# Attention and a squared-ReLU MLP in one kernel: the moving operands of both MLP products read as two interleaved halves

## Chip, cores, metric

The kernel runs on one NeuronCore of a Trainium2 chip. The metric is device time in microseconds, from one launch; what the host does before and after (turning arrays round, putting columns in order) is not in it.

## The reference

Two attention steps with 32 inducing points over 4 x 12480 tokens of 128 channels, then an MLP with 2048 hidden units on all 49920 tokens.

```python
def mab(q, kv):
    s = scale * (q @ kv.transpose(0, 2, 1))
    s = s - s.max(-1, keepdims=True)
    a = np.exp(s)
    a /= a.sum(-1, keepdims=True) + 1e-09
    return a @ kv
h = mab(I, x)
return mab(x, h).astype(np.float32)
...
h = x @ w_in
r = np.maximum(h, 0.0)
g = s * (r * r) + b
return (g @ w_out).astype(np.float32)
```

## The kernel before

The tokens are cut into 104 blocks of 480 (`BLK`; 26 for each of 4 batches). A token is a column, a channel a partition. The second attention step isn't multiplied out: `attend` leaves, for each block, the attention weights split into a high and a low float32r part and spread over 128 partitions (`a2t`), and `wst` holds the inducing points' values already multiplied by `w_in`, split in the same way. One product of `wst` (128 of 2048 hidden units at a time) with `a2t` then gives `h`.

**A pair** is two such products, 256 hidden units of one block, 8 pairs to a block, 832 in all. Its steps, each recorded at the line named:

- L737, TensorE: two matmuls `h <- a2t, wst` into one of three PSUM tiles `h` (two banks each). The moving operand is `a2t`, 480 columns.
- L752 (ScalarE) or L754 (VectorE): `r = relu(h)`, kept in SBUF.
- L802, ScalarE: `g1 = r * r`, rounded to float32r, for one pair (960 columns a partition) or for two at once (1920).
- L765, VectorE: the product `S = relu(h) * r` without that rounding. For a pair of kind "P" it goes to an SBUF tile `g`, for kind "D" back over `h` in PSUM.
- L779: `g2 = S - g1`, the rounding error of the square: on GpSimd for kind P, on VectorE for kind D.
- L827, TensorE: `x += w_hi * g1 + w_lo * g1` (four matmuls a pair) and `x += w_hi * g2` (two), into one of two banks `x` that collect a block. The moving operands are `g1` and `g2`, 480 columns each.
- L835 or L837: when a block is complete, scale and bias into `ob`, and a store.

In the names of the profile the buffer numbers are left out, so `g`, `g1` and `g2` all stand there as `g`. So both MLP products together are 104 x 16 x 4 = 6656 matmuls of 128 x 128 x 480, and each has its own weights loaded ahead of it.

**Work beside it.** While batch b's blocks run, the attention of batch b + 1 (`scores`, `top`, `values`, `points`, `w_tiles`) and the next `attend` are put between, at the block counts in `ATTEND_AT`, `SCORES_AT` and so on. They use the bank `x` that the running block does not.

**What sets the order.** `Plan` is a list scheduler that runs while the program is built. Each unit of work names its engine, its estimated time and an urgency; the constants at the top (`M_U`, `R_U`, `SQ`, `S_U`, `C_U`, `OUT_HI`, `OUT`) are added to a pair's number to make urgencies, `MM` is its estimate for one matmul, and `SLIP` and `WEIGHT` say how far urgency may hold an engine back. The order that comes out is fixed in the program. Kind P or D is also chosen there: a pair is P while the planner's backlog of GpSimd work is under `POOL_Q` and a tile `g` is free. Nothing is chosen on the chip.

**The opening** (up to about 61 us) does the first attention step for batch 0, brings in and narrows the weights, and keeps TensorE busy with warm-up matmuls (L959), whose results are not used. They run on a tile of zeros, with moving operands of eight forms, four matmuls each, in the order of the list `shapes`:

```python
plain = warm_sb[:, 0:BLK]
shapes = [
    plain,
    warm_sb.rearrange("p (t n) -> p n t", t=2)[:, 0:BLK // 2, :],
    warm_sb.rearrange("p (n t) -> p n t", t=2)[:, :, 0],
    warm_sb[:, 0:BLK // 2].unsqueeze(2).broadcast_to([P, BLK // 2, 2]),
    warm_sb.rearrange("p (t a c) -> p a t c", t=2, c=16)[:, 0:BLK // 32],
    warm_16[:, 0:BLK],
    warm_sb[:, 4:4 + BLK],
    warm_sb.rearrange("p (t a c) -> p a t c", t=2, c=4)[:, 0:BLK // 8],
]
```

The second form takes columns 0, 480, 1, 481 and so on; the last takes four columns from one half, then four from the other.

Of the kernel before, what the change touches and what calls it, by code (L numbers as in the profile page):

```python
# [9 lines left out]

F32 = mybir.dt.float32
F32R = mybir.dt.float32r
BF16 = mybir.dt.bfloat16
I32 = mybir.dt.int32
U32 = mybir.dt.uint32
AF = mybir.ActivationFunctionType
# [4 lines left out]
P = 128  # L21
T = 120
NQ = 4
BLK = T * NQ
# [3 lines left out]
TH = 8  # L28
WC = 512

POOL_Q = 4.228
POOL_L = 2.231


LAT = 0.180
SLIP = 0.159
WEIGHT = 0.0272
LEAN = {"ACT": -0.50}
R_LEAN = {"DVE": 0.00}


M_U = -5.604
R_U = 2.437
SQ = 3.369
MM = 0.2165
S_U = -1.313
C_U = -5.000
OUT_HI = 1.632
OUT = 1.982
FRONT = 0.379  # L50
FIRST = -200.0
SPREAD = -50.0
# [20 lines left out]
class Plan:  # L73
# [13 lines left out]
    def _step(self, unit, urgency, ready=None):  # L87
# [3 lines left out]
        if want is not None:  # L91
            eng, us, *waits = want
            if not isinstance(eng, dict):
                engs, lean = {eng: us}, LEAN
            elif isinstance(us, dict):
                engs, lean = eng, us
            else:
                engs, lean, waits = eng, LEAN, [us, *waits]
            more = sum(w for w in waits if isinstance(w, float))
# [16 lines left out]
    def run(self):  # L116
        ev = self.events
        while self.units:
            able = {}
            for u in self.units:  # L120
# [7 lines left out]
                )  # L128
                able.setdefault(eng, []).append((at + WEIGHT * urgency, at, engs[eng], u))
            assert able, [(u[3], u[4]) for u in self.units]  # L130
            picks = []
            for eng, steps in able.items():
                best = min(steps, key=lambda x: x[0])

                fill = [x for x in steps if x[1] + x[2] <= best[1] + SLIP]
                picks.append((*min(fill or [best], key=lambda x: x[0])[1:], eng))
# [8 lines left out]
def tile_attn_relu2(ctx: ExitStack, tc: tile.TileContext, xT, xN, indT, w_in, w_out, s_rep, b_rep, outT):  # L145
    nc = tc.nc
    B, _, N = xT.shape
# [23 lines left out]


    bank = [ps_x.tile([P, 512], F32, name=f"x{n}") for n in range(2)]

    def copy(out, in_):

        if plan.eng == "ACT":
            nc.scalar.copy(out=out, in_=in_)  # L178
        else:
            nc.vector.tensor_copy(out=out, in_=in_)  # L180
# [3 lines left out]
    def ring(name, bufs):  # L184

        n = taken.get(name, 0)
        taken[name] = n + 1
        if n < bufs:
            plan.events[name, n - bufs] = 0.0
        return n, (name, n - bufs)  # L190

    def next_free(name, bufs):

        n = taken.get(name, 0)
        return 0.0 if n < bufs else plan.events.get((name, n - bufs), math.inf)
# [522 lines left out]
    def place(k):  # L718
        blk, pr = divmod(k, NPAIR)
        return *divmod(blk, NBLK), pr  # L720
# [5 lines left out]
    def pair(k):  # L726

        b, blk, pr = place(k)
        n = pr % 2
        turn, free = ring("h", 3)  # L730
        yield "PE", 2 * MM, M_U, free, ("a2t", b, blk), ("wst", b, 2 * pr * P // WC), ("mm1", k - 1)
        wst, (A, A_turn) = st[b]["wst"], a2t[b, blk]
        h = ps_h.tile([P, 2, 512], F32, name="h")
        hv = h[:, :, 0:BLK]
        for u in range(2):
            c = 2 * pr + u
            nc.tensor.matmul(h[:, u, 0:BLK], wst[:, c * P:(c + 1) * P], A, start=True, stop=True)  # L737
        plan.set(("mm1", k))
        if pr == NPAIR - 1:
            plan.set(("a2t", A_turn))  # L740
        if k + 1 < total:
            plan.spawn(pair(k + 1), k + 1, plan.end)
        if n == 0:
            quad[k] = {"r": ring("r", 2), "g1": ring("g1", 4), "g1_uses": 4, "r_uses": 4, "R": []}
        q = quad[k - n]
        yield dict(ACT=0.855, DVE=1.08), R_LEAN, R_U, q["r"][1]
        if n == 0:
            q["r_t"] = ew.tile([P, 4, BLK], F32, name="r", bufs=2)
        half = slice(2 * n, 2 * n + 2)
        r = q["r_t"][:, half, :]  # L750
        if plan.eng == "ACT":
            nc.scalar.activation(out=r, in_=hv, func=AF.Relu)  # L752
        else:
            nc.vector.tensor_scalar(out=r, in0=hv, scalar1=0.0, scalar2=None, op0=ALU.max)  # L754
        plan.set(("R", k))
        q["R"].append((n, plan.end))
        if len(q["R"]) == 1:
            plan.spawn(square(k - n), k + SQ, plan.end + LAT)
        yield "DVE", 1.07, S_U
        wait = max(0.0, pool_work[0] - plan.end)  # L760
        kind = "P" if wait < POOL_Q and next_free("g", 4) <= plan.start else "D"
        if kind == "P":
            g_turn, _ = ring("g", 4)
        g = hv if kind == "D" else ew.tile([P, 2, BLK], F32, name="g", bufs=4)
        nc.vector.scalar_tensor_tensor(out=g, in0=hv, scalar=0.0, in1=r, op0=ALU.max, op1=ALU.mult)  # L765
        plan.set(("S", k))
        if kind != "D":
            plan.set(("h", turn))
        q["r_uses"] -= 1
        if q["r_uses"] == 0:  # L770
            plan.set(("r", q["r"][0]))
        if kind == "P":
            pool_work[0] = max(pool_work[0], plan.end) + POOL_L
        n2, free2 = ring("g2", 8)
        yield ("Pool", POOL_L, ("Q", k), free2) if kind == "P" else ("DVE", 1.07, C_U, ("Q", k), free2)
        hi = q["g1_t"][:, half, :]
        g2 = ew.tile([P, 2, BLK], F32R, name="g2", bufs=8)
        eng = nc.gpsimd if kind == "P" else nc.vector
        eng.tensor_tensor(out=g2, in0=g, in1=hi.bitcast(F32), op=ALU.subtract)  # L779
        plan.set(("h", turn) if kind == "D" else ("g", g_turn))  # L780
        g1_used(q)
        ops = [(w_hi[:, 2 * pr + u, :], g2[:, u, :]) for u in range(2)]
        plan.spawn(out_part(k, ops, 2 * MM, "w_split", lambda: plan.set(("g2", n2))), k + OUT, plan.end + LAT)

    def g1_used(q, n=1):
        q["g1_uses"] -= n
        if q["g1_uses"] == 0:
            plan.set(("g1", q["g1"][0]))

    def square(k0):  # L790
# [12 lines left out]
        for i in range(lo, hi):  # L803
# [3 lines left out]
            plan.spawn(  # L807
                out_part(k0 + i, ops, 4 * MM, "w_split", lambda: g1_used(q)), k0 + i + OUT_HI, plan.end + LAT
            )
        if q["R"]:  # L810
            plan.spawn(square(k0), k0 + 1 + SQ, q["R"][0][1] + LAT)
        q["r_uses"] -= hi - lo
# [3 lines left out]
    def out_part(k, ops, us, weights, used):  # L816

        b, blk, pr = place(k)
        blk_g = b * NBLK + blk
        yield "PE", us, (weights, 2 * pr * P // WC), ("front", blk_g - 1) if blk_g else "first", ("ob", blk_g - 2)  # L820
        o = bank[blk_g % 2][:, 0:BLK]
        left = parts.setdefault(blk_g, 2 * NPAIR)
        first = left == 2 * NPAIR
        left -= 1
        parts[blk_g] = left
        for n, (w, g) in enumerate(ops):
            nc.tensor.matmul(o, w, g, start=first and n == 0, stop=left == 0 and n == len(ops) - 1)  # L827
        used()
        if left:
            return  # L830
        front_work(blk_g + 1)
        yield dict(ACT=0.64, DVE=0.69), 0.0, "bias"
        ob = p2.tile([P, BLK], F32, name="ob")
        if plan.eng == "ACT":
            nc.scalar.activation(out=ob, in_=o, func=AF.Identity, bias=bias, scale=s_sb)  # L835
        else:
            nc.vector.tensor_scalar(out=ob, in0=o, scalar1=s_sb, scalar2=bias, op0=ALU.mult, op1=ALU.add)  # L837
        c0 = b * N + blk * BLK
        nc.sync.dma_start(out=outT[:, c0:c0 + BLK], in_=ob)
        plan.set(("ob", blk_g))  # L840
# [68 lines left out]
    left = [0, 0, 0]  # L909
# [7 lines left out]
    def opening():  # L917
# [18 lines left out]
    warm_turn, _ = ring("g2", 8)  # L936
    warm_sb = ew.tile([P, 2 * BLK], F32R, name="g2", bufs=8)
    nc.gpsimd.memset(warm_sb.bitcast(F32), 0.0)
    warm_16 = warm_sb.bitcast(BF16)
    plain = warm_sb[:, 0:BLK]  # L940
    shapes = [
        plain,
        warm_sb.rearrange("p (t n) -> p n t", t=2)[:, 0:BLK // 2, :],
        warm_sb.rearrange("p (n t) -> p n t", t=2)[:, :, 0],
        warm_sb[:, 0:BLK // 2].unsqueeze(2).broadcast_to([P, BLK // 2, 2]),
        warm_sb.rearrange("p (t a c) -> p a t c", t=2, c=16)[:, 0:BLK // 32],
        warm_16[:, 0:BLK],
        warm_sb[:, 4:4 + BLK],
        warm_sb.rearrange("p (t a c) -> p a t c", t=2, c=4)[:, 0:BLK // 8],
    ]  # L950
    shapes = itertools.cycle([x for x in shapes for _ in range(4)])

    def warm(n, ps, *waits):

        for _ in range(n):
            yield "PE", 0.22, *waits
            x = next(shapes)
            w = (warm_16 if x.dtype == BF16 else warm_sb)[:, 0:P]
            nc.tensor.matmul(ps()[:, 0:BLK], w, x, start=True, stop=True)  # L959

    def keep_warm(ps, *waits):

        while plan.events.get(("a2t", 0, 0), math.inf) > plan.end + 0.3:
            yield from warm(1, ps, *waits)
        plan.set(("g2", warm_turn))
# [27 lines left out]
_OUT = "out_dram"  # L993
# [33 lines left out]
```

## Time and profile before

| | |
|---|---|
| median of 3 runs | 1614.33 us (1614.32 to 1616.04) |
| profiled execution | 1615.43 us, its span 1613.6 us |
| granted TensorE clock | 0.998 of full speed |
| matmuls of L737 / L827 | 1664 / 4992 |
| pairs of kind P / D | 682 / 150 |
| relus on ScalarE / VectorE | 661 / 171 |
| squares of one pair / of two | 808 / 12 |

The span runs from the first to the last instruction of the profiled execution, so a sum made from its rows is a sum for that execution. In the rows below a group's two numbers behind the bar are its busy time in us and the mean of one in ns; behind the second bar stands the engine's idle time just before the group, and what ended most of it. Matmuls overlap, so their mean (380 ns) is not their pace; the pace is the distance between starts. PE is TensorE, DVE VectorE, ACT ScalarE, POOL GpSimd.

### The profile page before, as it was taken

The numbers are of one execution on the slowest core, as the hardware profiler recorded it, in microseconds if no ns is written. First come the engines' busy times: TensorE is split into PE (matmuls) and PEld (weight loads), VectorE is DVE, ScalarE is ACT, GpSimd is POOL, SyncE is SP. The second block draws the span as 40 slices with busy tenths as digits, with TensorE's granted clock in tenths as the row PEclk, the third lists the DMA queues.
The fourth block names the chain that finished last, engine by engine and source line by source line (L and its number), as shares of the span: only waits on it lengthen the run. The fifth ranks groups of instructions, "written<-read, shape, count | busy, mean of one in ns | idle before, by whom it ended". The sixth has DMA issues, their size and how long they took to land.

```text
span 1613.6 us, 24901 instructions
## 1 busy us (share of the span) xinstructions
PE 1596.5 (99%) x8223; PEld 1300.7 (81%) x8223; DVE 1462.3 (91%) x1590; ACT 1514.9 (94%) x1812; POOL 1541.4 (96%) x701
## 2 busy tenths in 40 slices
PE   8899999999999999999999999999999999999998
PEld 5578788888887878888887788888888888888787
DVE  5899999989999999999999989989998999998996
ACT  7599999999999999999999999999999999999997
POOL 1699999999999999999999999999999999999998
PEclk9999999999999999999999999999999999999999
DMA  8222313313233222231223322322311112112100
GB/s 299 64 89 89 104 62 117 99 40 89 63 104 101 70 88 91 90 103 52 74 92 99 100 84 74 117 80 62 92 46 62 38 49 68 31 52 66 56 31 19
DMA packets 59312, 129.42 MB, mean 80 GB/s; under 512 B 11952, under 2 KB 38576, under 8 KB 59184
## 3 DMA queue, kind: packets, MB, share of 16 engines
q1 hardware_dynamic: 59184, 127.83, 25.2%
q8 instruction: 67, 1.10, 0.3%
q14 instruction: 61, 0.50, 0.1%
HBM read 73.52 MB, written 25.56 MB: 61 GB/s over the span
## 4 chain that ended last, share of the span: by engine, by line
PE 96%; ACT 1%; DVE 1%; DMA 0%; issue 0%; POOL 0%; POOLq 0%; SPq 0%; ACTq 0%
PE x L827 67%; PE h L737 23%; PE x L662 2%; PE x L612 1%; PE x L573 1%; DMA xt<-in_xT_dram 0%; PE h L959 0%; PE h L414 0%; PE x L362 0%; ACT r L752 0%; PE h L382 0%; POOL g L779 0%; ACT e L392 0%; DVE g L765 0%; PE h L397 0%
## 5 line engine op out<-in xcount | busy, mean ns | idle before, releaser
L779 POOL TENSOR_TENSOR g<-g,g 128x960 fp32r<-128x960 f32 x682 | 1523.7, 2293 | 18.6 <-DVE g L765 12.0
L827 PE MATMUL x<-g,w_hi 128*128 128x480 f32 x3328 | 1058.7, 381 | 1.5 <-POOL g L779 1.5
L765 DVE SCALAR_TENSOR_TENSOR g<-h,r 128x960 f32<-128x960 f32 x682 | 768.1, 1147 | 61.7 <-ACT r L752 50.6
L802 ACT ACTIVATE g<-r 128x960 fp32r<-128x960 f32 x820 | 806.8, 1016 | 18.3 <-DVE r L754 4.7
L827 PEld LDWEIGHTS x<-g,w_hi 128*128 128x128 f32 x3328 | 622.8, 188 | 113.5 <-POOL g L779 9.3
L752 ACT ACTIVATE r<-h 128x960 f32<-128x960 f32 x661 | 626.8, 967 | 43.6 <-PE h L737 29.2
L827 PE MATMUL x<-g,w_lo 128*128 128x480 f32 x1664 | 633.1, 380 | 2.4 <-ACT g L802 1.5
L737 PE MATMUL h<-a2t,wst 128*128 128x480 f32 x1664 | 505.7, 385 | 0.5 <-DVE g L765 0.3
L737 PEld LDWEIGHTS h<-a2t,wst 128*128 128x128 f32 x1664 | 305.4, 188 | 85.6 <-issue 28.4
L827 PEld LDWEIGHTS x<-g,w_lo 128*128 128x128 f32 x1664 | 312.6, 188 | 56.2 <-issue 4.9
L754 DVE TENSOR_SCALAR r<-h 128x960 f32<-128x960 f32 x171 | 196.6, 1150 | 19.8 <-PE h L737 16.8
L765 DVE SCALAR_TENSOR_TENSOR h<-h,r 128x960 f32<-128x960 f32 x150 | 173.7, 1158 | 9.4 <-ACT r L752 8.6
L779 DVE TENSOR_TENSOR g<-h,g 128x960 fp32r<-128x960 f32 x150 | 172.6, 1151 | 7.9 <-ACT g L802 2.4
L835 ACT ACTIVATE ob<-x,bias,s_sb 128x480 f32<-128x480 f32 x103 | 77.0, 748 | 9.4 <-PE x L827 8.7
L310 POOL TENSOR_TENSOR w_in_sb<-w_in_sb,g 128x512 f32<-128x512 f32 x4 | 5.3, 1333 | 26.0 <-DVE g L305 26.0
L662 PE MATMUL x<-xt,hT 128*32 128x480 f32 x208 | 28.3, 578 | 0.5 <-DVE hT L501 0.5
L694 DVE TENSOR_TENSOR hl<-x,hl 128x480 fp32r<-128x480 f32 (+1 forms) x28 | 18.3, 655 | 7.3 <-ACT hl L178 6.7
L310 POOL TENSOR_TENSOR wst<-wst,g 128x512 f32<-128x512 f32 x4 | 5.8, 1466 | 19.1 <-DVE g L305 19.1
L612 PEld LDWEIGHTS x<-xn,eT 128*32 128x32 f32 (+1 forms) x630 | 16.9, 109 | 7.0 <-DVE eT L607 3.7
L612 PE MATMUL x<-xn,eT 128*32 128x128 f32 (+1 forms) x630 | 22.5, 275 | 0.0
L669 DVE STREAM_TRANSPOSE x<-x 128x480 f32<-128x480 f32 (+1 forms) x28 | 19.3, 690 | 3.4 <-PE x L662 3.3
L573 PE MATMUL x<-xt,ind_sb 128*32 128x480 f32 x156 | 21.2, 578 | 0.0
(116 smaller groups left out, 417.8 us busy)
## 6 DMA issues: line engine op xcount, KB each, us to landing
xt<-in_xT_dram SPq DMA_DIRECT2D x102, 480.0 KB, 4.4
a2t<-hl SPq DMA_DIRECT2D x416, 60.0 KB, 2.0
out_dram<-ob SPq DMA_DIRECT2D x104, 240.0 KB, 2.0
xn<-in_xN_dram SPq DMA_DIRECT2D x18, 512.0 KB, 3.8
xn<-in_xN_dram SPq DMA_DIRECT2D x18, 448.0 KB, 4.4
wst<-whl SPq DMA_DIRECT2D x48, 64.0 KB, 2.0
g<-in_w_in_dram SPq DMA_DIRECT2D x4, 512.0 KB, 6.6
g<-in_w_out_dram SPq DMA_DIRECT2D x4, 512.0 KB, 5.9
```

The lines of the kernel that those rows point to most:

```text
L573: nc.tensor.matmul(ps[M * q:M * (q + 1), 0:BLK], ind_sb, xt[:, q % SB], start=True, stop=True)
L612: nc.tensor.matmul(ps[M * c:M * (c + 1), 0:P], eT[0:rows, n], xn_tiles[b, g, half][0][0:rows, n - half * TH], start=n < P // M, stop=n + P ...
L662: nc.tensor.matmul(ps[M * q:M * (q + 1), 0:BLK], hT[:, 0:M], xt[:, q % SB], start=True, stop=True)
L669: nc.vector.transpose(out=s, in_=s)
L737: nc.tensor.matmul(h[:, u, 0:BLK], wst[:, c * P:(c + 1) * P], A, start=True, stop=True)
L752: nc.scalar.activation(out=r, in_=hv, func=AF.Relu)
L754: nc.vector.tensor_scalar(out=r, in0=hv, scalar1=0.0, scalar2=None, op0=ALU.max)
L765: nc.vector.scalar_tensor_tensor(out=g, in0=hv, scalar=0.0, in1=r, op0=ALU.max, op1=ALU.mult)
L779: eng.tensor_tensor(out=g2, in0=g, in1=hi.bitcast(F32), op=ALU.subtract)
L802: nc.scalar.activation(out=q["g1_t"][:, sl, :], in_=q["r_t"][:, sl, :], func=AF.Square)
L827: nc.tensor.matmul(o, w, g, start=first and n == 0, stop=left == 0 and n == len(ops) - 1)
L835: nc.scalar.activation(out=ob, in_=o, func=AF.Identity, bias=bias, scale=s_sb)
```

## The change

A function `by_turns` reads a tile of 480 columns as two halves by turns: columns 0, 240, 1, 241, and so on. It is put around the moving operand of both products. The result is written without gaps, so `h` has its columns in the new order, and `x` in that order applied twice; everything between works column by column. The host undoes it twice on the output. Besides, the planner's constants have new values, and the warm-up matmuls run through six other forms (40 of them, not 41). Lines behind L176 have numbers 3 higher in the changed kernel (L737 becomes L740, L765 L768, L779 L782, L802 L805, L827 L830).

```diff
-POOL_Q = 4.228
+POOL_Q = 2.9681
...
-SLIP = 0.159
-WEIGHT = 0.0272
-LEAN = {"ACT": -0.50}
-R_LEAN = {"DVE": 0.00}
+SLIP = 0.0319
+WEIGHT = 0.0251
+LEAN = {"ACT": -0.5}
+R_LEAN = {"DVE": -0.008}
...
-SQ = 3.369
-MM = 0.2165
...
-C_U = -5.000
-OUT_HI = 1.632
-OUT = 1.982
+SQ = 1.2698
+MM = 0.2035
...
+C_U = -11.5827
+OUT_HI = 1.9705
+OUT = 0.5153
...
+    def by_turns(x):
+
+        return x.rearrange("p (t n) -> p n t", t=2)
...
-            nc.tensor.matmul(h[:, u, 0:BLK], wst[:, c * P:(c + 1) * P], A, start=True, stop=True)
+            nc.tensor.matmul(h[:, u, 0:BLK], wst[:, c * P:(c + 1) * P], by_turns(A), start=True, stop=True)
...
-            nc.tensor.matmul(o, w, g, start=first and n == 0, stop=left == 0 and n == len(ops) - 1)
+            nc.tensor.matmul(o, w, by_turns(g), start=first and n == 0, stop=left == 0 and n == len(ops) - 1)
...
-    return np.ascontiguousarray(r.results[0][_OUT].T)
+    y = r.results[0][_OUT]
+    for _ in range(2):
+        y = y.reshape(C, B * N // BLK, BLK // 2, 2).transpose(0, 1, 3, 2).reshape(C, B * N)
+    return np.ascontiguousarray(y.T)
```

The new constants move instructions. On VectorE, in the middle of the program, around the end of one `attend` (the transposition of `x`, then `hl`) and a `values` (`eT`, `accb`), the order before is:

```order
L687 STREAM_TRANSPOSE x_86<-x_86 128x480
L765 SCALAR_TENSOR_TENSOR g<-h,r 128x960
L694 TENSOR_TENSOR hl<-x_86,hl 128x480
L765 SCALAR_TENSOR_TENSOR g<-h,r 128x960 x3
L607 STREAM_TRANSPOSE eT<-s 128x480
L754 TENSOR_SCALAR r<-h 128x960
L765 SCALAR_TENSOR_TENSOR g<-h,r 128x960
L623 TENSOR_TENSOR accb<-x_85,accb 128x128
L765 SCALAR_TENSOR_TENSOR g<-h,r 128x960 x2
L765 SCALAR_TENSOR_TENSOR h<-h,r 128x2x480
```

At the same place in the changed kernel, on the same engine:

```order
L690 STREAM_TRANSPOSE x_86<-x_86 128x480
L768 SCALAR_TENSOR_TENSOR g<-h,r 128x960
L697 TENSOR_TENSOR hl<-x_86,hl 128x480
L768 SCALAR_TENSOR_TENSOR g<-h,r 128x960 x2
L757 TENSOR_SCALAR r<-h 128x960
L610 STREAM_TRANSPOSE eT<-s 128x480
L768 SCALAR_TENSOR_TENSOR g<-h,r 128x960
L768 SCALAR_TENSOR_TENSOR h<-h,r 128x2x480
L626 TENSOR_TENSOR accb<-x_85,accb 128x128
L782 TENSOR_TENSOR g_7094<-h,g_7054 128x960
```

Behind the transposition seven products went to `g`, for GpSimd, ahead of the first that stays in `h`; now it is four, and VectorE makes that pair's difference itself (L782). Over the whole program 659 pairs are P and 173 D.

On ScalarE, the end of the program before:

```order
L752 ACTIVATE r<-h 128x960 x2
L802 ACTIVATE g_16089<-r 128x960
L802 ACTIVATE g_16131<-r 128x960
L752 ACTIVATE r<-h 128x960
L802 ACTIVATE g_16131<-r 128x960
L835 ACTIVATE ob<-x_86,bias,s_sb 128x480
```

And in the changed kernel:

```order
L838 ACTIVATE ob<-x_85,bias,s_sb 128x480
L805 ACTIVATE g_16059<-r 128x960
L755 ACTIVATE r<-h 128x960 x2
L805 ACTIVATE g_16059<-r 128x960
L805 ACTIVATE g_16089<-r 128x1920
L838 ACTIVATE ob<-x_86,bias,s_sb 128x480
```

The last two pairs' squares are one instruction of 1920 columns now. Over the program 37 squares are of two pairs and 758 of one (12 and 808 before); ScalarE has 678 relus (661) and VectorE 154 (171).

On TensorE, the last matmuls before, all of L827:

```order
L827 MATMUL x_86<-g_16131,w_lo 128x480
L827 MATMUL x_86<-g_16131,w_hi 128x480
L827 MATMUL x_86<-g_16153,w_hi 128x480 x2
L827 MATMUL x_86<-g_16165,w_hi 128x480 x2
L827 MATMUL x_86<-g_16169,w_hi 128x480 x2
```

And in the changed kernel:

```order
L830 MATMUL x_86<-g_16095,w_hi 128x480 x2
L830 MATMUL x_86<-g_16104,w_hi 128x480 x2
L830 MATMUL x_86<-g_16089,w_lo 128x480
L830 MATMUL x_86<-g_16089,w_hi 128x480
L830 MATMUL x_86<-g_16089,w_lo 128x480
L830 MATMUL x_86<-g_16089,w_hi 128x480
L830 MATMUL x_86<-g_16114,w_hi 128x480 x2
L830 MATMUL x_86<-g_16110,w_hi 128x480 x2
```

Before, three differences of GpSimd (`g_16153`, `g_16165`, `g_16169`) came last. Now two of the last ones are VectorE's (`g_16104`, `g_16114`), and one of GpSimd (`g_16110`) still ends the program.

More of the change, by code (lines that the diff above doesn't have):

```diff
@@ L12 @@
 F32R = mybir.dt.float32r
-BF16 = mybir.dt.bfloat16
 I32 = mybir.dt.int32
@@ L29 @@
 WC = 512
-POOL_Q = 4.228
+POOL_Q = 2.9681
 POOL_L = 2.231
 LAT = 0.180
-SLIP = 0.159
-WEIGHT = 0.0272
-LEAN = {"ACT": -0.50}
-R_LEAN = {"DVE": 0.00}
-M_U = -5.604
-R_U = 2.437
-SQ = 3.369
-MM = 0.2165
-S_U = -1.313
-C_U = -5.000
-OUT_HI = 1.632
-OUT = 1.982
+SLIP = 0.0319
+WEIGHT = 0.0251
+LEAN = {"ACT": -0.5}
+R_LEAN = {"DVE": -0.008}
+M_U = -6.4309
+R_U = 1.8519
+SQ = 1.2698
+MM = 0.2035
+S_U = -1.1474
+C_U = -11.5827
+OUT_HI = 1.9705
+OUT = 0.5153
 FRONT = 0.379
@@ L938, in tile_attn_relu2 @@
     nc.gpsimd.memset(warm_sb.bitcast(F32), 0.0)
-    warm_16 = warm_sb.bitcast(BF16)
-    plain = warm_sb[:, 0:BLK]
     shapes = [
[L942 to L949, printed above, removed]
+        warm_sb[:, 0:BLK].rearrange("p (n t) -> p t n", t=2),
+        warm_sb.rearrange("p (n t) -> p t n", t=2)[:, 0],
+        warm_sb[:, 0:BLK].rearrange("p (t n) -> p n t", t=4),
+        warm_sb[:, 0:BLK].rearrange("p (t n) -> p n t", t=BLK // 4),
+        warm_sb[:, 0:BLK].rearrange("p (t a c) -> p a t c", t=2, c=2),
+        by_turns(warm_sb[:, 0:BLK]),
     ]
@@ L957, in warm @@
             x = next(shapes)
-            w = (warm_16 if x.dtype == BF16 else warm_sb)[:, 0:P]
-            nc.tensor.matmul(ps()[:, 0:BLK], w, x, start=True, stop=True)
+            nc.tensor.matmul(ps()[:, 0:BLK], warm_sb[:, 0:P], x, start=True, stop=True)
     def keep_warm(ps, *waits):
```

## The prediction

> **What bounds the kernel now.** I read the page first, then the long stretch without the opening, then the groups, then single stretches of the time line.
>
> ```profile
> span 1613.6 us, 24901 instructions
> PE 1596.5 (99%) x8223; PEld 1300.7 (81%) x8223; DVE 1462.3 (91%) x1590; ACT 1514.9 (94%) x1812; POOL 1541.4 (96%) x701
> PE 96%; ACT 1%; DVE 1%; DMA 0%; issue 0%; POOL 0%; POOLq 0%; SPq 0%; ACTq 0%
> ...
> core 0: us, PE busy (x) PEld busy (x) DVE busy (x) ACT busy (x) POOL busy (x), PEclk, DMA share, GB/s
> 61.00:1613.60 1552.60, 1544.42 (x7692) 1267.53 (x7690) 1422.19 (x1495) 1476.49 (x1713) 1526.18 (x684) 1.00 0.24 75
> ```
>
> The reader is to see two things. The chain that ended last is TensorE's, 96%. And behind it stands not one idle engine but a second one that is nearly full: from 61 us on GpSimd works 1526.2 of 1552.6 us, 98%. TensorE can gain only until GpSimd becomes the end. DMA, at a share of 0.24, is far off, and the granted clock is 1.00, so no throttle hides in the numbers.
>
> A busy TensorE is not a TensorE at its peak, so I take its pace from where matmuls follow each other without a wait, in the chain of waits:
>
> ```profile
> 467.31 3.49 PE x L827 x16
> 1237.51 4.78 PE x L827 x22
> ```
>
> 3.49 / 16 = 0.2181 and 4.78 / 22 = 0.2173 us: **0.218 us for one product of 480 columns** with a plainly read moving operand.
>
> **The price of the new reading** stands in this trace already, because the warm-up matmuls (L959) take eight forms of moving operand in turn, four of each, in the order of the list `shapes`. The last 13 of the 41, numbers 29 to 41, run in one piece ahead of the first pair. By the list they are four that read runs of 4 columns by turns from two places, four plain, four that take single columns by turns from two halves, and one with a stride of 2. In the chain of waits, then in the time line (start, time until the last one's end, count):
>
> ```profile
> 57.99 3.29 PE h L959 x13
> ...
> 58.32 0.85 PE L959 MATMUL h<-g 128*128 128x480 f32 x3
> ...
> 59.01 1.04 PE L959 MATMUL h<-g 128*128 128x480 f32 x4
> ...
> 59.88 0.97 PE L959 MATMUL h<-g 128*128 128x480 f32 x4
> ...
> 60.69 0.59 PE L959 MATMUL h<-g 128*128 128x480 f32 x1
> ```
>
> The first line is all 13; the others begin with numbers 30, 33, 37 and 41. From start to start: runs of 4, (59.01 - 58.32) / 3 = 0.230; plain, (59.88 - 59.01) / 4 = 0.2175, the pace of the main part; single columns by turns, (60.69 - 59.88) / 4 = **0.2025 us**. Against the 0.218 of the main part that is 0.0155 us less for each.
>
> What these rows don't show is the exact form of the change: there the halves lie 480 columns apart, here 240, and the tiles hold data, not zeros. I bound it by the same rows, 0.2025 below and 0.230 above, and take 0.2025, since the order of reading (one column from either half) is that of the 0.2025 row, and since plain reads cost the same on zeros (0.2175) and on data (0.218). Both ends count for the range.
>
> The Trainium skill, page "SBUF — State Buffer", section "Door 1: The DMA port swizzle", speaks against the change: SBUF has lines of 16 bytes, an access runs at full speed only with two or more hits in a line, and every step to another line is paid for. By that rule a read that changes lines at every column is the worst form of all; here it is the fastest of the three. For this form the trace disagrees with the page.
>
> **Term 1, TensorE.** Both products make 1664 + 3328 + 1664 = 6656 matmuls (L737 and the two rows of L827 in the groups below). 6656 x 0.0155 = 103 us. If TensorE stayed the end, the span would be 1613.6 - 103 = 1510.6 us.
>
> **Term 2, the other engines.** The change sets the planner's numbers anew, and so shares out the elementwise work differently. The rows that price it:
>
> ```profile
> L779 POOL TENSOR_TENSOR g<-g,g 128x960 fp32r<-128x960 f32 x682 | 1523.7, 2293 | 18.6 <-DVE g L765 12.0 <-PE x L827 2.6 <-ACT hl L178 1.1
> L827 PE MATMUL x<-g,w_hi 128*128 128x480 f32 x3328 | 1058.7, 381 | 1.5 <-POOL g L779 1.5
> L802 ACT ACTIVATE g<-r 128x960 fp32r<-128x960 f32 x808 | 785.2, 1004 | 18.1 <-DVE r L754 4.7 <-issue 0.4
> L765 DVE SCALAR_TENSOR_TENSOR g<-h,r 128x960 f32<-128x960 f32 x682 | 768.1, 1147 | 61.7 <-ACT r L752 50.6 <-POOL g L779 6.9
> L827 PE MATMUL x<-g,w_lo 128*128 128x480 f32 x1664 | 633.1, 380 | 2.4 <-ACT g L802 1.5 <-DVE hl L694 0.8
> L752 ACT ACTIVATE r<-h 128x960 f32<-128x960 f32 x661 | 626.8, 967 | 43.6 <-PE h L737 29.2 <-ACT g L802 9.8 <-ACT r L752 1.9
> L737 PE MATMUL h<-a2t,wst 128*128 128x480 f32 x1664 | 505.7, 385 | 0.5 <-DVE g L765 0.3
> L754 DVE TENSOR_SCALAR r<-h 128x960 f32<-128x960 f32 x171 | 196.6, 1150 | 19.8 <-PE h L737 16.8 <-ACT r L752 1.3 <-ACT g L802 0.5
> L765 DVE SCALAR_TENSOR_TENSOR h<-h,r 128x960 f32<-128x960 f32 x150 | 173.7, 1158 | 9.4 <-ACT r L752 8.6
> L779 DVE TENSOR_TENSOR g<-h,g 128x960 fp32r<-128x960 f32 x150 | 172.6, 1151 | 7.9 <-ACT g L802 2.4
> L802 ACT ACTIVATE g<-r 128x1920 fp32r<-128x1920 f32 x12 | 21.8, 1816 | 0.2
> ```
>
> Counted over the whole program in the order of the changed kernel:
> - GpSimd makes 659 differences in place of 682. One costs 1523.7 / 682 = 2.234 us, so 23 x 2.234 = **51.4 us less**: 1526.2 becomes 1474.8.
> - Those 23 go to VectorE (173 in place of 150), which also makes 154 relus, not 171: 23 x 1.151 - 17 x 1.150, with 23 products that now end in PSUM (1.158 for 768.1 / 682 = 1.126), an `ob` and a copy: about +9, so 1422.2 becomes 1431.
> - ScalarE takes the 17 relus (17 x 0.948 = +16.1). 758 single and 37 double squares replace 808 and 12: -50 x 0.972 + 25 x 1.816 = -3.2. With the `ob` and copy that leave, 1476.5 becomes 1488.
>
> By busy time ScalarE would now be ahead of GpSimd, but its busy time shrinks when it is pressed: an isolated operation counts with its latency, one of a row does not.
>
> ```profile
> 700.02 1.82 ACT L752 ACTIVATE r<-h 128x960 f32<-128x960 f32 x2
> 1599.76 1.90 ACT L802 ACTIVATE g<-r 128x960 fp32r<-128x960 f32 x2
> ```
>
> Two relus take 1.82, less one of 0.967: 0.853 us apart. Squares: 1.90 - 1.004 = 0.896. At that spacing the work is 678 x 0.853 + 758 x 0.896 + 37 x 1.71 (estimated as 1.816 less the same 0.11) = 1321, and 1462 with the other 141 us. GpSimd has no such reserve: 682 operations in 1523.7 us already stand in a row. So the order of needs from 61 us on is GpSimd 1475, ScalarE 1462, then TensorE 1552.6 - 103 = 1450, VectorE 1431 at most. **GpSimd becomes the end.**
>
> **Where GpSimd begins and ends** (stretches of the time line):
>
> ```profile
> 65.45 2.25 POOL L779 TENSOR_TENSOR g<-g,g 128x960 fp32r<-128x960 f32 x1
> 67.66 1.29 POOL L320 TENSOR_TENSOR w_lo<-wst,w_hi 128x512 fp32r<-128x512 f32 x1
> ...
> 1606.75 2.26 POOL L779 TENSOR_TENSOR g<-g,g 128x960 fp32r<-128x960 f32 x1
> 1609.06 0.70 PE L827 MATMUL x<-g,w_hi 128*128 128x480 f32 x2 [1.47 <-POOL g L779]
> 1609.81 0.75 ACT L835 ACTIVATE ob<-x,bias,s_sb 128x480 f32<-128x480 f32 x1 [6.25 <-PE x L827]
> ```
>
> From its first difference at 65.45 to its last end at 1609.01 are 1543.6 us: 1523.7 busy, 18.6 idle, 1.3 for L320. Ahead of it lies the opening, in which the changed order moves only warm-up matmuls (40, not 41; 12 at another 0.0155 or so, 0.2 us, taken as nothing). Behind it lie two matmuls, one `ob` and one store: 4.6 us. The changed order ends in the same way, on a GpSimd difference and two matmuls, so the tail stays.
>
> The sum: 65.45 + 659 x 2.234 + 1.3 + 18.6 + 4.6 = **1562 us of span**, 51.4 less than 1613.6. The profiled execution took 1615.43 us in all; the median of the three runs, 1614.33, lies 0.7 us above its span. I add these 0.7: 1563. So of the 103 us that TensorE could give, only the 51 stay by which GpSimd's work shrinks. The idle 18.6 us is the chosen term: I keep it, because GpSimd was fed as tightly before, and because its largest part (12.0, waiting for VectorE) came from a chain that starts with the wait for TensorE's `h`, which gets shorter. What covers it is the queue of up to four `g` tiles; the planner now hands GpSimd a pair only while its backlog is under 2.97 us (4.23 before), so this cover is thinner. Idle of 4 us gives 1548, and nothing goes below 1544.
>
> **Rivals.**
>
> **ScalarE and the queues between engines set the end.** All four engines would be over 91% full, which is where small waits add up.
>
> ```profile
> DVE g L765 <- ACT r L752: 50.6, 84, 1.8
> ACT r L752 <- PE h L737: 29.2, 57, 2.1
> POOL g L779 <- DVE g L765: 12.0, 19, 2.0
> ACT ob L835 <- PE x L827: 8.7, 7, 6.2
> ```
>
> ScalarE was idle 1552.6 - 1476.5 = 76.1 us. Only its waits for TensorE go, 29.2 + 8.7 less the 6.2 of the last block: 31.7. If the other 44.4 stay and no busy time shrinks, 61 + 1488 + 44.4 = 1593.5, or 1594. For it: VectorE waits for ScalarE's relu most of all. Against it: the spacing above. Chance 0.13.
>
> **Part of the gain.** At a spacing between 0.2025 and 0.210 nothing changes, since 6656 x 0.0077 = 51 us already brings TensorE level with GpSimd. Between 0.210 and 0.218 TensorE stays the end and the time lies between 1563 and 1614; 1590 at 0.2145. Chance 0.07.
>
> **The change doesn't do what it says.** If columns 240 apart are read as plain ones, TensorE stays at 1613.6 and the time at 1614: the removed GpSimd work was not on its path. Chance 0.04. The Trainium skill, page "TensorE: Matmul & The Clock Gate", section "Wait — 56ns, not 53.3ns?", gives N / 2.4 GHz plus about 2.5 ns, 202.5 ns at 480 columns, for any warm matmul; then plain reading would have nothing to gain. The trace disagrees on the plain reads (0.2175) and has the page's figure only where columns are taken by turns.
>
> **Slower: the halves collide.** If a distance of 240 columns costs what runs of 4 cost, 0.230, then 6656 x 0.012 = 80 us come on top and TensorE ends at 1613.6 + 80 = 1694. It decides from any spacing above 0.218. For it: of the forms with turns one is slower than plain. Against it: that form also changes places only every fourth column, and the one that matches the change is fastest. Chance 0.06.
>
> **How the numbers follow.** Forecast 0.70, at 1563. The range takes in GpSimd idle of 4 us below and the ScalarE case above: 1548 to 1595, which with the greater part of the rival of 0.07 holds over 0.8; what is left out is no gain, and slower. About 0.2% (3 us) is what a measurement of this kernel can tell from no change. Faster by more: 0.70 + 0.13 + 0.07 = 0.90; within: 0.04; slower: 0.06.
>
> **What would show it.** Starts of neighbouring matmuls in L740 and L830 stand 0.2025 us apart (0.218 or more: the price is wrong). GpSimd has 659 differences at 2.23 us and idles under 25 us behind 65 us; if it idles 50, the ScalarE rival holds, and ScalarE's idle time names whom it waits for. TensorE, now some 45 us short of work, waits for L782 and for ScalarE, and the chain that ended last is no longer TensorE's alone. If TensorE still fills 99% with few waits, the reading, not the sharing, was misjudged.

## The result, and the profile after

| | before | changed |
|---|---|---|
| median | 1614.32 us (4 runs, 1614.03 to 1616.04) | 1555.78 us (4 runs, 1554.71 to 1556.5) |
| ratio | | 0.9635, 95% interval 0.9618 to 0.9651 |
| profiled execution, its span | 1615.43, 1613.6 us | 1555.31, 1553.5 us |

The forecast was 1563 us, within 1548 to 1595. The page of the changed kernel: span, busy time by engine, and the chain that ended last by engine and by line.

```profile
span 1553.5 us, 24873 instructions
...
PE 1521.2 (98%) x8222; PEld 1295.1 (83%) x8222; DVE 1463.2 (94%) x1598; ACT 1505.0 (97%) x1802; POOL 1471.5 (95%) x678
...
PE 74%; ACT 13%; DVE 6%; issue 5%; POOL 1%; ACTq 0%; DVEq 0%; POOLq 0%
PE x L830 50%; PE h L740 18%; ACT g L805 6%; ACT r L755 5%; DVE g L768 3%; PE x L576 1%; PE x L615 1%; PE h L957 1%; PE x L665 1%; ACT ob L838 1%; POOL g L782 1%; PE x L365 0%; DVE h L768 0%; ACT hl L181 0%; DVE hl L697 0%
```

TensorE's share of the chain fell from 96% to 74%. What came in is ScalarE (13%) and VectorE (6%). GpSimd, which the forecast named as the new end, has 1%. From 61 us on, by engine:

```profile
core 0: us, PE busy (x) PEld busy (x) DVE busy (x) ACT busy (x) POOL busy (x), PEclk, DMA share, GB/s
61.00:1553.50 1492.50, 1467.38 (x7696) 1261.85 (x7694) 1422.04 (x1502) 1465.47 (x1702) 1455.76 (x661) 1.00 0.25 78
```

TensorE, ScalarE and GpSimd all stand at 98% of these 1492.5 us. The pace of the matmuls, from long pieces of the chain of waits (start, length, count):

```profile
94.07 3.24 PE x L830 x16
...
120.53 3.24 PE x L830 x16
...
1542.36 7.30 PE x L830 x36
```

3.24 / 16 = 0.2025 us, where it was 0.218. The last line is the end of the program: 36 matmuls in one run. So it was TensorE with work in hand that ended it, not a wait for the last difference of GpSimd. The groups, with idle time behind the second bar:

```profile
L782 POOL TENSOR_TENSOR g<-g,g 128x960 fp32r<-128x960 f32 x659 | 1453.3, 2249 | 27.0 <-DVE g L768 13.2 <-ACT g L805 8.0 <-PE h L740 1.3
...
L755 ACT ACTIVATE r<-h 128x960 f32<-128x960 f32 x678 | 637.9, 972 | 6.3 <-PE h L740 3.2 <-ACT r L755 1.7 <-DVE g L768 0.2
...
L740 PE MATMUL h<-a2t,wst 128*128 128x480 f32 x1664 | 488.9, 376 | 11.6 <-DVE g L768 9.1 <-DVE g L782 1.3
```

ScalarE's relu, which idled 43.6 us before, mostly for `h`, idles 6.3. The waits have turned round: TensorE now waits for VectorE to free a tile `h`. And one GpSimd difference takes 1453.3 / 659 = 2.205 us, not 2.234, though nothing in its own instruction changed.

### The profile page after: what moved, and what is told of

The parts are those of the page before. It is cut to its first block, busy times and chain, and to the rows that moved or that the text cites. A ratio compares the mean times of both kernels' runs of the same rounds, so it can differ in the third digit from the quotient of the medians.

```text
span 1553.5 us, 24873 instructions
## 1 busy us (share of the span) xinstructions
PE 1521.2 (98%) x8222; PEld 1295.1 (83%) x8222; DVE 1463.2 (94%) x1598; ACT 1505.0 (97%) x1802; POOL 1471.5 (95%) x678
## 4 chain that ended last, share of the span: by engine, by line
PE 74%; ACT 13%; DVE 6%; issue 5%; POOL 1%; ACTq 0%; DVEq 0%; POOLq 0%
PE x L830 50%; PE h L740 18%; ACT g L805 6%; ACT r L755 5%; DVE g L768 3%; PE x L576 1%; PE x L615 1%; PE h L957 1%; PE x L665 1%; ACT ob L838 1%; POOL g L782 1%; PE x L365 0%; DVE h L768 0%; ACT hl L181 0%; DVE hl L697 0%
## 5 line engine op out<-in xcount | busy, mean ns | idle before, releaser
L782 POOL TENSOR_TENSOR g<-g,g 128x960 fp32r<-128x960 f32 x659 | 1453.3, 2249 | 27.0 <-DVE g L768 13.2
L830 PE MATMUL x<-g,w_hi 128*128 128x480 f32 x3328 | 1046.2, 367 | 5.2 <-POOL g L782 3.7
L805 ACT ACTIVATE g<-r 128x960 fp32r<-128x960 f32 (+1 forms) x795 | 798.0, 1046 | 12.4 <-DVE r L757 3.2
L768 DVE SCALAR_TENSOR_TENSOR g<-h,r 128x960 f32<-128x960 f32 x659 | 742.5, 1146 | 28.2 <-ACT r L755 21.9
L830 PEld LDWEIGHTS x<-g,w_hi 128*128 128x128 f32 x3328 | 625.2, 189 | 67.7 <-POOL g L782 15.8
L755 ACT ACTIVATE r<-h 128x960 f32<-128x960 f32 x678 | 637.9, 972 | 6.3 <-PE h L740 3.2
L830 PE MATMUL x<-g,w_lo 128*128 128x480 f32 x1664 | 611.5, 367 | 2.7 <-ACT g L805 1.6
L740 PE MATMUL h<-a2t,wst 128*128 128x480 f32 x1664 | 488.9, 376 | 11.6 <-DVE g L768 9.1
L740 PEld LDWEIGHTS h<-a2t,wst 128*128 128x128 f32 x1664 | 295.5, 189 | 101.1 <-issue 40.3
L830 PEld LDWEIGHTS x<-g,w_lo 128*128 128x128 f32 x1664 | 314.4, 189 | 31.9 <-DVE hl L697 4.1
L782 DVE TENSOR_TENSOR g<-h,g 128x960 fp32r<-128x960 f32 x173 | 199.6, 1155 | 14.0 <-ACT g L805 4.0
L768 DVE SCALAR_TENSOR_TENSOR h<-h,r 128x960 f32<-128x960 f32 x173 | 200.1, 1157 | 5.6 <-ACT r L755 5.1
L757 DVE TENSOR_SCALAR r<-h 128x960 f32<-128x960 f32 x154 | 176.9, 1150 | 7.4 <-PE h L740 5.4
```

What stands on the lines that cost most here:

```text
L805: nc.scalar.activation(out=q["g1_t"][:, sl, :], in_=q["r_t"][:, sl, :], func=AF.Square)
L830: nc.tensor.matmul(o, w, by_turns(g), start=first and n == 0, stop=left == 0 and n == len(ops) - 1)
```

## The experiments

Two questions: what does the reading do and what the new order, and who sets the end of the changed kernel. Ratios are to the kernel before, run on the same chip.

### Reading and order apart

Old order, new reading:

```diff
-nc.tensor.matmul(h[:, u, 0:BLK], wst[:, c * P:(c + 1) * P], A, start=True, stop=True)
+nc.tensor.matmul(h[:, u, 0:BLK], wst[:, c * P:(c + 1) * P], by_turns(A), start=True, stop=True)
...
-nc.tensor.matmul(o, w, g, start=first and n == 0, ...)
+nc.tensor.matmul(o, w, by_turns(g), start=first and n == 0, ...)
...
```

The part left out puts the columns back on the host.

> The kernel before with its own constants and order, and only the two moving operands read by turns (the host puts the columns back). All theories: neighbouring matmuls 0.2025 us apart. GpSimd has 682 differences. Theory A (how TensorE reads is what made a GpSimd difference shorter, 2.234 to 2.205 us): 65.5 + 682 x 2.205 + 1.3 + 19 to 27 idle + 4.6 = 1594 to 1602 us of span. Theory B (the new order and sharing made it shorter): 2.234 stays, 1613 to 1621, so no gain at all from the reading alone.

New order, old reading (the changed kernel, with its warm-up forms, without `by_turns` in the two products):

> The changed kernel with its constants, order and warm-up forms, but both products read plainly. All theories: matmuls 0.218 us apart, TensorE the end again, 1614 to 1630 us. Theory A: a GpSimd difference takes 2.234 us again. Theory B: it stays at 2.205 although TensorE reads plainly.

Measured:

| | old order | new order |
|---|---|---|
| plain reading | 1615.69 | 1625.99, 1.0066 (1.0051 to 1.0081) |
| by turns | 1576.48, 0.9762 (0.9746 to 0.9779) | 1555.78, 0.9635 (0.9618 to 0.9651) |

The last field is from the first comparison, with its own runs of before. The reading alone is worth 39 us, the order alone costs 10 (2.8 of them in the opening, where the first pair begins at 63.86 us in place of 61.10). Together they are worth 59: the new order pays 21 us only where matmuls are fast. Both expectations for the reading alone missed: theory B said 1613 to 1621, and theory A 1594 to 1602, since it kept 19 to 27 us of GpSimd idle. GpSimd's row in that run:

```profile
L783 POOL TENSOR_TENSOR g<-g,g 128x960 fp32r<-128x960 f32 x682 | 1499.6, 2268 | 3.3 <-DVE g L769 2.9 <-ACT r L756 0.2
```

It idled 3.3 us, and a difference took 1499.6 / 682 = 2.199 us in the old order as well. So theory A's other half held: the reading makes GpSimd faster, not the order. With the new order and plain reading it is slow again:

```profile
L782 POOL TENSOR_TENSOR g<-g,g 128x960 fp32r<-128x960 f32 x659 | 1476.3, 2282 | 72.5 <-DVE g L768 32.8 <-ACT g L805 28.0 <-PE h L740 6.0
```

### One product at a time

The changed kernel with `by_turns` left in L740 only, then in L830 only:

> The changed kernel with only the first product (L740) read by turns, the second plainly. TensorE: 1664 matmuls at 0.2025 and 4992 at 0.218, 77 us more than in the changed kernel (TensorE's 1441 from 61 us on become 1518): TensorE the end, 1585 to 1600 us. Theory A: a GpSimd difference near 2.23 us, since three quarters of the reads are plain. Theory B: 2.205.

> The changed kernel with only the second product (L830) read by turns, the first plainly. TensorE: 1664 matmuls at 0.218, 26 us more (1441 become 1467). If GpSimd alone sets the end of the changed kernel, these 26 us cost little: 1556 to 1562. If TensorE shares in the end (the rival of small waits that add up): 1570 to 1582. Theory A: a GpSimd difference a quarter of the way from 2.205 to 2.234, 2.21.

Measured: 1602.5 us, 0.9920 (0.9906 to 0.9935), and 1566.97 us, 0.9701 (0.9687 to 0.9716); the first a little above its 1585 to 1600, the second between what either view allowed. For GpSimd, the median distance between the starts of differences that follow each other without a pause, over each trace:

| matmuls read plainly | kernel | us |
|---|---|---|
| all 6656 | before | 2.231 |
| all 6656 | order alone | 2.231 |
| 4992 | first product by turns | 2.222 |
| 1664 | second product by turns | 2.207 |
| none | changed | 2.200 |
| none | reading alone | 2.198 |

It follows the share of plain reads and not the order: theory A. And 26 us more for TensorE (second product alone by turns) cost 11 us, 77 more (first alone) cost 47. An engine that set the end alone would pass on all, one that had no part in it, nothing. So TensorE shares the end. One thing moves along with it in these runs: GpSimd's differences get longer too, by 659 x 0.007 = 5 us and 659 x 0.022 = 14 us in all. In the next run half of GpSimd's work goes, and the end of the changed kernel stays where it is.

### Who holds the end: one engine lighter at a time

Same order, same reading, and one engine relieved of more work than the others could follow. GpSimd first:

```diff
-eng.tensor_tensor(out=g2, in0=g, in1=hi.bitcast(F32), op=ALU.subtract)
+m = 1 if kind == "P" else 2
+eng.tensor_tensor(out=g2[:, 0:m], in0=g[:, 0:m], in1=hi[:, 0:m].bitcast(F32), op=ALU.subtract)
...
```

> The changed kernel in the same order, but each GpSimd difference makes only the first 480 of 960 columns (the matmuls use these twice; the second half of the correction is left out). GpSimd then has over 600 us less to do. Theory GpSimd (it alone sets the end of the changed kernel): the time falls until the next engine holds it, by 30 us or more, to 1525 or below. Theory all (the four engines and the waits between them share the end): it falls by no more than GpSimd's idle-free share of the chain, under 15 us, 1541 to 1553.

TensorE:

```diff
-for u in range(2) for w in (w_lo, w_hi)]
+for u in range(2) for w in (w_hi, w_lo)]
...
-nc.tensor.matmul(o, w, by_turns(g), ...)
+lo = len(ops) == 4 and n % 2
+x = by_turns(g)[:, 0:BLK // 4] if lo else by_turns(g)
+nc.tensor.matmul(o[:, 0:BLK // 2] if lo else o, w, x, ...)
```

> The changed kernel in the same order, but the w_lo products of the squares run over 240 of 480 columns, after the w_hi one instead of ahead of it (the rest of that product is left out). TensorE has 1664 x 0.1 = 166 us less to do. Theory GpSimd: the time falls by less than 5 us. Theory all: it falls by 10 to 25 us, to 1531 to 1546, since GpSimd's 1453 us and ScalarE stop it there.

ScalarE and VectorE:

```diff
-nc.scalar.activation(out=r, in_=hv, func=AF.Relu)
+nc.scalar.activation(out=r[:, 0], in_=hv[:, 0], func=AF.Relu)
...
```

> The changed kernel in the same order, but ScalarE's 678 relus make 480 of 960 columns and later steps read these twice (half of the hidden units' values are replaced by the other half's). ScalarE has about 678 x 0.4 = 270 us less to do. Theory GpSimd: under 5 us less. Theory all: 8 to 25 us less, 1531 to 1548.

```diff
-nc.vector.scalar_tensor_tensor(out=g, in0=hv, scalar=0.0, in1=r, op0=ALU.max, op1=ALU.mult)
+nc.vector.scalar_tensor_tensor(out=g[:, 0], in0=hv[:, 0], scalar=0.0, in1=r[:, 0], op0=ALU.max, op1=ALU.mult)
...
```

> The changed kernel in the same order, but VectorE's 832 products S make 480 of 960 columns and the difference reads these twice (the other half is left out). VectorE has about 832 x 0.5 = 416 us less to do. Theory GpSimd: under 5 us less. Theory all: 8 to 25 us less, 1531 to 1548; VectorE is the emptiest of the four, so the least of the three.

| relieved | us | ratio to before | against the 1555.78 of the changed kernel |
|---|---|---|---|
| GpSimd | 1555.49 | 0.9626 (0.9599 to 0.9654) | -0.3 |
| TensorE | 1546.35 | 0.9570 (0.9542 to 0.9598) | -9.4 |
| VectorE | 1545.15 | 0.9563 (0.9535 to 0.9590) | -10.6 |
| ScalarE | 1536.65 | 0.9510 (0.9482 to 0.9538) | -19.1 |

Each ratio's interval is about 4 us to either side, so GpSimd's can't be told from nothing, nor TensorE's from VectorE's. Theory GpSimd falls. With half the work its row has 791.8 us of work and 685.7 of idle time, for the same end.

```profile
L783 POOL TENSOR_TENSOR g<-g,g 128x480 fp32r<-128x480 f32 x659 | 791.8, 1212 | 685.7 <-DVE g L768 340.3 <-ACT g L806 245.4 <-PE x L831 22.8
```

The other three each give something, and little beside what was taken from them: an estimated 166 us from TensorE, and by busy time from 61 us on 377 from VectorE (1422 to 1045) and 226 from ScalarE (1465 to 1239). They hand the end to each other, which is theory all for these three; its sizes missed in part: it gave GpSimd 1541 to 1553, TensorE at most 1546, and VectorE the least of the three. The halved relus and products S also return the tiles `h` sooner, so these runs don't tell an engine's time from the turnaround of `h`. With ScalarE relieved, the chain is TensorE's to 87%:

```profile
PE 87%; DVE 7%; issue 3%; ACT 2%; POOL 2%; DVEq 0%; ACTq 0%; POOLq 0%
```

Then both at once, the ScalarE edit and the TensorE edit together:

> The changed kernel with ScalarE's relus halved (the hidden units' values of one half stand for the other's) and the w_lo products of the squares over 240 of 480 columns: both reliefs at once. Theory S (ScalarE and TensorE hold the end together, GpSimd stands next): below either relief alone (1536.7 and 1546.4), down to where GpSimd holds it, 66.2 + 659 x 2.200 + 1.2 + 0 to 10 idle + 5.1 = 1522 to 1533. Theory V (VectorE and the three tiles h hold it as much): no lower than 1534.

1523.0 us, 0.9424 (0.9407 to 0.9441): 32.8 us less, about as much as the two reliefs apart (28.5, each with some 4 us to either side). It lies where theory S put it, and theory V's "no lower than 1534" falls, though the halved relus free the tiles `h` sooner here too. Here GpSimd does hold it, and its row shows what that looks like:

```profile
L782 POOL TENSOR_TENSOR g<-g,g 128x960 fp32r<-128x960 f32 x659 | 1448.0, 2266 | 0.7 <-DVE g L768 0.3 <-DVE x L683 0.2
...
PEld x L833 <- POOL g L782: 117.4, 237, 1.9
```

0.7 us of idle time, and TensorE's weight loads waiting 117 us for it (15.8 in the changed kernel). So GpSimd's floor lies some 33 us under the changed kernel.

### Was GpSimd the end with the old sharing?

The same halving, in the kernel with the reading alone:

> The kernel of the run with the reads alone (old constants and order), but each GpSimd difference makes 480 of 960 columns (the matmuls use these twice; half of the correction is left out). Theory G (with the old sharing GpSimd set the end): the time falls from 1576.5 to between 1545 and 1562, to where the other three engines hold it, about as in the changed kernel. Theory O (the old order as such is slow): it stays within 5 us of 1576.5.

1570.54 us, 0.9718 (0.9700 to 0.9736): 5.9 us less. The fall that theory G named, to 1545 to 1562, didn't come, and theory O missed by 0.9 us.

```profile
L784 POOL TENSOR_TENSOR g<-g,g 128x480 fp32r<-128x480 f32 x682 | 818.9, 1212 | 677.1 <-DVE g L769 384.2 <-ACT g L807 189.4 <-PE x L832 20.6
```

Both theories held in part. In the kernel with the reading alone GpSimd did set the end: its first difference starts at 66.0 us, then come 1499.6 of work, 1.3 for the one other operation, 3.3 of idle time, and a tail of 4.5 behind the last difference, together the span of 1574.7 us. But without half that work the other engines, in the old order, hold the end only 6 us lower, at a span of 1568.4. So the 21 us that the new order gains with fast matmuls need two things. With 682 differences of this length GpSimd alone fills the span up to about 1571 us, however the rest is ordered, so the 23 differences had to leave it; and taking work off GpSimd brings no more than 6 us unless the other engines' work is placed and shared differently too. How the 21 us divide between the two isn't shown, and which of the planner's numbers does the second was not tried.

### The reading itself

The changed kernel with 152 warm-up matmuls of 16 forms at its start:

```diff
+def turns(d):
+    return one.rearrange("p (a t c) -> p a c t", t=2, c=d)
...
+for x, cols in probes:
+    for _ in range(8):
+        yield "PE", 0.22, *waits
+        nc.tensor.matmul(ps()[0:cols, 0:BLK], warm_sb[:, 0:cols], x, start=True, stop=True)
```

> The changed kernel with 152 warm-up matmuls ahead of everything, eight of each form, in place of the first six: its own time is some 30 us longer and says nothing; the distance between matmuls of a form is what is asked. Weights of 128 columns where nothing is said. Plain: 0.218 us. By turns from columns 240 apart: 0.2025. What makes the plain read slow? Theory W (it collides with the load of the next weights): plain with weights of 32 columns, whose load is a quarter as long, falls to 0.2025 to 0.207. Theory R (the read itself): it stays at 0.218. What makes the turns fast? Theory T (any two places 16 bytes or more apart): distances 120, 48, 16, 8 and 4 columns all 0.2025, and distance 2, which stays within four columns, 0.218. Theory D (the distance itself decides): they differ, some at 0.218 or more. Quarters by turns 0.255, pairs of columns by turns 0.306 and all even columns before the odd ones 0.427, as in the changed kernel's opening; sixths by turns above 0.255.

Its time line, cut so that a row begins with a form (start, time to the last one's end, count). In turn: plain; plain with weights of 32 columns, from the second on; halves 240 apart by turns; then 41 with the last of those, the same with 32-column weights, and distances 120, 48, 16 and 8; distance 4; distance 2; sixths by turns; quarters by turns; pairs of columns from two halves; the even columns before the odd ones.

```profile
9.26 1.89 PE L970 MATMUL h<-g 128*128 128x480 f32 x8
...
11.20 1.66 PE L970 MATMUL h<-g 128*32 128x480 f32 x7
...
12.70 1.78 PE L970 MATMUL h<-g 128*128 128x480 f32 x8
...
14.12 8.47 PE L970 MATMUL h<-g 128*128 128x480 f32 x41
...
22.42 1.78 PE L970 MATMUL h<-g 128*128 128x480 f32 x8
...
24.04 1.90 PE L970 MATMUL h<-g 128*128 128x480 f32 x8
...
25.78 2.38 PE L970 MATMUL h<-g 128*128 128x480 f32 x8
...
27.98 2.20 PE L970 MATMUL h<-g 128*128 128x480 f32 x8
...
30.02 2.62 PE L970 MATMUL h<-g 128*128 128x480 f32 x8
...
32.48 3.62 PE L970 MATMUL h<-g 128*128 128x480 f32 x8
```

From the distance between starts (the last of the nine steps in the first row belongs to 32-column weights):

| form | us for one |
|---|---|
| plain | (11.20 - 9.26) / 9 = 0.2156 |
| plain, 32-column weights | (12.70 - 11.20) / 7 = 0.214 |
| two places by turns, 240 to 8 columns apart | (22.42 - 14.12) / 41 = 0.2024 |
| two places 4 apart | (24.04 - 22.42) / 8 = 0.2025 |
| two places 2 apart | (25.78 - 24.04) / 8 = 0.2175 |
| six places by turns | (27.98 - 25.78) / 8 = 0.275 |
| four places by turns | (30.02 - 27.98) / 8 = 0.255 |
| pairs of columns | (32.48 - 30.02) / 8 = 0.3075 |
| even, then odd columns | 0.43 (3.62, less 0.6 for the last one's own length, over 7) |

Theory T holds for the distances tried, theory D falls: from 4 columns (16 bytes) to 240 the distance is the same to TensorE, and at 2 the turns gain nothing. Theory W explains little of the plain read's price, about 0.002 of 0.013. The test is weaker than it was meant to be, since the load of 32 columns took 0.109 us in this trace and that of 128 columns 0.189, so it was not a quarter as long. That most of the price is the read itself (R) is likely, not shown.

### The warm-up forms

One part of the change made the opening longer, its warm-up forms. Here all warm-up matmuls take the fast form.

```diff
-shapes = [
-    warm_sb[:, 0:BLK].rearrange("p (n t) -> p t n", t=2),
...
-]
+shapes = [by_turns(warm_sb[:, 0:BLK])]
```

> The changed kernel with all warm-up matmuls read by turns from halves 240 columns apart, the form that takes 0.2025 us, in place of six forms of up to 0.43. In the changed kernel the last 13 of them ended 1.45 us later than before, and TensorE's first pair began at 62.55 us in place of 61.10. Theory: the first pair at 61.0 to 61.2 us and 1.0 to 1.6 us less in all, 1554.2 to 1554.8. Rival: the opening doesn't hold the end, since the 1.4 us are caught up behind it: 1555.8.

The first pair's row, in the changed kernel and in this one:

```profile
62.55 1.40 PE L740 MATMUL h<-a2t,wst 128*128 128x480 f32 x6
```

```profile
60.92 1.38 PE L740 MATMUL h<-a2t,wst 128*128 128x480 f32 x6
```

TensorE's pairs begin 1.6 us earlier and the profiled span is 1552.1 us, 1.4 less than the changed kernel's 1553.5, whose own runs spread by 1.8. The median is 1553.48, ratio 0.9611 (0.9598 to 0.9624). This leans towards the theory; by the ratios, whose intervals overlap, the two kernels can't be told apart.

The form isn't all of it. A stretch of the last warm-up matmuls in the kernel before, in the changed kernel and in this one, with the granted clock third from the right:

```profile
58.00:61.00 3.00, 3.00 (x13) 2.55 (x14) 2.97 (x4) 0.08 (x1) 0.00 (x0) 1.00 0.35 86
...
58.40:61.50 3.10, 3.10 (x9) 2.48 (x8) 1.88 (x3) 1.15 (x2) 0.00 (x0) 0.50 0.39 97
...
57.00:60.00 3.00, 3.00 (x9) 2.56 (x8) 2.63 (x4) 0.64 (x2) 0.00 (x0) 0.50 0.39 95
```

At a clock of 0.50 the four by quarters of the changed kernel stand 0.400 us apart, not 0.255, and nine of this kernel's matmuls by turns also 0.400, not 0.2025. So the clock cost this opening time as well; why it fell there and not in the kernel before isn't shown.

## Why the prediction was right, and where it wasn't

The time lay in the range and 7 us under the point. But the step that gave the point, **"GpSimd becomes the end"**, is wrong for this kernel, and so is its conclusion that only the 51 us stay by which GpSimd's work shrinks. Relieving GpSimd of half its work changed nothing that can be measured (-0.3 us). It is right for the kernel with the reading alone, where GpSimd idles 3.3 us. That the point still came near is in part luck, as the bookkeeping below shows.

- **The price of the reading** was right: 0.2025 us, found in four warm-up matmuls of the trace before. The unknown, 240 columns apart in place of 480 and data in place of zeros, made no difference. The text says that the trace has 202.5 ns only where columns are taken by turns. That overlooks four warm-up matmuls of bf16 in the same trace (numbers 21 to 24, from 54.25 us on): read straight on, with weights of bf16 too, the last two starts stand 0.202 and 0.203 us behind the one before.
- **Term 2's order of needs** failed in how it was read. GpSimd 1475, ScalarE 1462, TensorE 1450 and VectorE 1431 lie within 3% of each other. Such a list doesn't name an end. The likely reason, not tested by itself, is that engines that wait for each other through three tiles `h` add their small waits before any of them is full. Of these four, the one with the largest sum was the only one whose relief brought nothing.
- **The rival "ScalarE and the queues between engines set the end"**, at a chance of 0.13, had more of the mechanism: ScalarE's relief gains the most, with TensorE and VectorE beside it. Its price was wrong, 1594 us. It kept 44.4 us of ScalarE idle, of which 1492.5 - 1465.5 = 27.0 are left, and 1488 us of busy time, which came to 1465.5. The count at back-to-back spacing, which the prediction itself makes, had said 1462.
- **The bookkeeping on GpSimd** came near by errors that cancelled: 659 x (2.205 - 2.234) = -19.1 us, idle time 27.0 in place of 18.6 (+8.4), a start at 66.85 in place of 65.45 (+1.4), a tail of 5.1 in place of 4.6 (+0.5). Together -8.8, from 1562.2 to the 1553.5 of the trace. It adds up because every engine works nearly to the end; that isn't the same as setting it. The floor, "nothing goes below 1544", was too high: with a difference at 2.200 us, the run with both reliefs ends at a span of 1520.8 us with the same 659 differences.
- **The signs**: matmuls 0.2025 us apart and a shared chain came. GpSimd idled 27.0 us, just over the 25 named and far from the 50 of the ScalarE rival, and TensorE was 25 us short of work (1492.5 - 1467.4), not 45.
- **The warm-up at nothing** was off by 1.4 us: the slow forms among them (0.43 us for even and odd columns apart) stood ahead of the first pair, and the granted clock there was 0.50.
- **The reading not doing what it says, and the halves colliding**: neither came up. By the Trainium skill, page "SBUF — State Buffer", section "Door 1: The DMA port swizzle", each step to another 16-byte line is paid for. Here 16 bytes are indeed where the time changes, but with two lines by turns it is the other way: that is the cheapest read.

## What to carry to other kernels

When several engines stand at 95% or more, the largest estimate of work doesn't name the end. The idle time that is left to an engine (3.3 us where GpSimd set the end, 27.0 where it didn't), the chain of waits and a run with one engine relieved tell more. A faster pace of one engine can pay more with an order made for it (59 us in place of 39, of the 103 that TensorE could give), and such an order can be slower by itself, as here by 0.7%. Where float32r columns stream into TensorE without order mattering, reading two places by turns, 16 bytes or more apart, is worth trying; other forms can cost twice as much (0.43 against 0.2025 us).

## What the hardware showed that I had not expected

- A moving operand of 480 float32r columns takes 0.2025 us when two places are read by turns, 0.216 when read straight on, 0.255 and 0.275 with four and six places, 0.3075 with pairs, 0.43 with a stride of two, all at a granted clock of 1.00. Why a straight read is slower than two places by turns isn't shown by any run; that bf16 columns read straight on take 0.2025 too is one more thing that an explanation has to fit.
- How TensorE reads slows GpSimd: a difference of two SBUF tiles takes 2.231 us beside plain reads and 2.200 beside reads by turns, with two values between for a quarter and three quarters of them. That the two share something in SBUF is a guess; no run shows by what way one slows the other.
